# Attention steps of 16 heads: both halves' logits together, products with v next, fill work last; a reordered program start

## The chip, the cores and the metric

The kernel runs on one core of one Trainium2 chip. The metric is device time in microseconds (us) from a single launch, the median of several executions. On one core there is no other die to compare with, so a run counts as fast when it is within 1.5% of the fastest run of the same kernel. The engines are called TensorE (PE in the profile), PEld (TensorE's weight loads), VectorE (DVE), ScalarE (ACT), GpSimd (POOL) and SyncE (SP, used here to issue DMAs). "L405" in a profile line is line 405 of that kernel's file.

## The reference

Four residual layers, A B A B, on 2048 rows of 576 features. Layer A is attention with 32 heads of 18 features; each query sees 8 keys, at distances 0, 2, ..., 14 behind it. Layer B is a gated MLP with a 2048 x 2048 spatial product; the change does not touch it.

```python
def _A_ref(x, wqkv, wo):
    B, S, D = x.shape                      # 1, 2048, 576
    H, W, dil = 32, 8, 2
    qkv = (x @ wqkv).reshape(B, S, 3, H, D // H).transpose(2, 0, 3, 1, 4)
    q, k, v = qkv[0], qkv[1], qkv[2]
    # ... idx = pos - off*dil, masked where negative; kg, vg are gathered keys and values
    logits = jnp.einsum('bhsd,bhswd->bhsw', q, kg) * (D // H) ** -0.5
    attn = softmax(where(mask, logits, -1e9))
    o = jnp.einsum('bhsw,bhswd->bhsd', attn, vg)
    return o.transpose(0, 2, 1, 3).reshape(B, S, D) @ wo

x = A_x
x = x + _A_ref(_layernorm(x), A_wqkv, A_wo)
x = x + _B_ref(_layernorm(x), B_w_in, B_w_sp, B_b_sp, B_w_out)
x = x + _A_ref(_layernorm(x), A_wqkv, A_wo)
x = x + _B_ref(_layernorm(x), B_w_in, B_w_sp, B_b_sp, B_w_out)
```

## The kernel before

Queries are worked in 19 "head-tiles" of up to 112 rows. For each one the kernel multiplies a window of keys with all queries of the tile for every head (the *logits*, with the window pattern packed into the contracted rows, so that the mask comes out of the same matmul), exponentiates the result on ScalarE, and multiplies it with v (the *products*). A ones column in v gives the softmax denominator. The logits matmuls of a head use 32 of the array's 128 rows; the four row groups are written `tile_position=(32*j, 0)`.

The unit of work is a half-step `u` of 8 heads: four of them make a head-tile, and there are 76 in one attention stage. The rest of the attention stage is *fill work*, put by a table between the half-steps: q and k projections (`PG`), v projections (`VW`), output projections (`WO`), layer norms, DMA issues. All engines run in the order in which the program is written here.

```python
def H_tile(self, name):                    # the logits' PSUM tile: two of them
    return self.ps.tile([P, 2, 512], f32, name=name, tag="H", bufs=2)
# ...
def VW(t, hh, dve):                        # v projection and its copy out of PSUM
    nk = tdim(t)[0]
    pv = self.PT_tile([P, 512], f32, "pv", any_bank=False)
    for c in range(5):
        nc.tensor.matmul(pv[:nk, 0:288], lhsT=self.xnT[:, c, QT * t:QT * t + nk],
                         rhs=wv_sb[:, c, hh * 288:(hh + 1) * 288], start=(c == 0), stop=(c == 4))
    evac(v_ext[:nk, t, ...], pv[:nk, 0:288], dve)       # dve: VectorE, else ScalarE
# ...
def L_mm(u):                               # logits of 8 heads into one H tile
    t, hf, jp = half(u)
    L_tiles[u] = L_ps = self.H_tile("L_ps")
    for ftl in range(4):
        for jj in range(2):
            j = 2 * jp + jj                # two of the four row groups
            nc.tensor.matmul(L_ps[:nk, jj, ...], lhsT=kT[32*j:32*j+32, ...], rhs=qT[32*j:32*j+32, ...],
                             start=True, stop=True, tile_position=(32 * j, 0))
# EXP(u): one activation on ScalarE, H tile -> P_bufs[u % 4]
# PV(u): 8 products with v, P_bufs[u % 4] -> O_ps; NORM(u): divide by the denominator (VectorE)
# ...
for t in range(nvw, NT):
    at(4 * t - 4, VW, t, 0, True)          # copy on VectorE
    at(4 * t - 3, VW, t, 1, False)         # copy on ScalarE
# ... PG, WO, layer norms and loads are placed by at() too
L_mm(0)
for u in range(NU):                        # NU = 76
    EXP(u)
    if u + 1 < NU:
        L_mm(u + 1)
    for f, a in table.pop(u, []):          # fill work
        f(*a)
    if u >= 1:
        PV(u - 1)
        if u % 2 == 0:
            NORM(u - 1)
```

At the program's start, GpSimd makes an identity matrix first (for transposes on TensorE), then a window pattern is built, stored on GpSimd's DMA queue and loaded back on ScalarE's, and the layer norms of rows 1024 to 1535 (the "third group") are applied before the first q and k projections. The q and k projections land in a staging tile and go from there into `QK` by DMA, alternating between the GpSimd and the SyncE queue.

The softmax here doesn't subtract the row's maximum and nothing guards it: scores larger than these inputs give would overflow.

## Time and profile before

| | before |
|---|---|
| time, median of 4 runs | 1252.67 us (1252.26 to 1254.16) |
| span of the profiled run, mean granted clock | 1250.7 us, 0.996 |
| TensorE busy | 1204.0 us (96%) |
| first attention stage, first logits to first MLP matmul | 111.1 us |
| second attention stage | 108.5 us |
| first q/k projection, first logits | 21.77 us, 52.67 us |
| TensorE waits, logits for exponentials | 11.6 us in 31 waits |

From the page of the kernel before: each engine's busy time (with share and number of instructions), the granted TensorE clock in tenths for 40 slices of the span, and the chain of waits by engine.

```profile
PE 1204.0 (96%) x8428; PEld 647.5 (52%) x8528; DVE 542.2 (43%) x1202; ACT 388.4 (31%) x609; POOL 277.6 (22%) x371
...
PEclk9899999999999999999999999999999999999999
...
PE 86%; POOL 3%; ACT 3%; issue 3%; DVE 2%; DMA 1%; SPq 1%; POOLq 0%; ACTq 0%; DVEq 0%
```

TensorE bounds the kernel, at nearly full clock. What matters is therefore whether a change gives TensorE less to do or makes it wait.

The waits of TensorE in the kernel before. A line reads: engine, tile and line that waited, what released it, then the total in us, the number of waits and the longest.

```profile
PE L_ps L405 <- ACT P_sb L413: 11.6, 31, 0.8
PE pt L514 <- DVE ln_xn L509: 10.5, 1, 10.5
PE pp L380 <- DMA xnT<-ln_xn: 4.0, 1, 4.0
PE pt L514 <- ACT xnT L516: 3.1, 1, 3.1
```

The attention loop costs TensorE very little waiting: 11.6 us in both stages together. The other three lines are the start: the first transpose runs at 10.5 us, then 3.1 us are lost to a ScalarE copy, and 4.0 us at the end of the start to transposed x.

The loop itself, in the timeline of TensorE in the kernel before. Columns: start in us, length in us, engine, line, operation, output and input by the program's names, their shapes, the number of instructions in the group.

```profile
711.02 0.78 PE L453 MATMUL pw<-wo_sb,oT 128*128 128x288 bf16 x5
711.63 0.35 PE L424 MATMUL O_ps<-v_ext,P_sb 128*128 128x19 bf16 x8
711.92 0.37 PE L405 MATMUL L_ps<-QK 32*128 32x112 bf16 x8
712.22 0.79 PE L358 MATMUL pv<-wv_sb,xnT 128*128 128x288 bf16 x5
```

There are no idle times in brackets, so there are no waits in this piece. A half-step's logits take 0.30 us until the next matmul starts, its products 0.29 us.

ScalarE in the same stage of the kernel before, where the copies of v alternate between the engines. Square brackets hold the idle time before the group and what ended it.

```profile
720.03 0.40 ACT L352 CAST v_ext<-pv 128x288 bf16<-128x288 f32 x1 [0.42 <-PE pv L358]
720.33 3.41 ACT L413 ACTIVATE P_sb<-L_ps 128x896 bf16<-128x896 f32 x4
725.12 0.40 ACT L352 CAST v_ext<-pv 128x288 bf16<-128x288 f32 x1 [1.38 <-PE pv L358]
```

Once per head-tile ScalarE stands up to 1.38 us idle until a v projection is ready to be copied, and then does four exponentials in a row. The period of 5.09 us from copy to copy is TensorE's, not ScalarE's.

Last, the groups of the logits (L405) and the products (L424) in the kernel before: shapes, count, busy us, mean ns of one, idle time before the group and its releasers. The busy times of two groups overlap where one starts before the other has ended (eight logits last 0.37 us, the next matmul starts after 0.30), so they can't be added up exactly.

```profile
L405 PE MATMUL L_ps<-QK 32*128 32x112 bf16 (+1 forms) x1216 | 54.9, 208 | 11.9 <-ACT P_sb L413 11.6
L424 PE MATMUL O_ps<-v_ext,P_sb 128*128 128x19 bf16 (+1 forms) x1216 | 53.8, 172 | 0.0
```

### The profile page before, as it was taken

The page shows a single profiled execution, that of the slowest core. Times are in us where ns is not written, and L with a number is a line of the kernel's source. Part 1 is how long each engine was busy: PE and PEld are TensorE (multiplying, and loading weights), DVE is VectorE, ACT ScalarE, POOL GpSimd, SP SyncE. Part 2 cuts the span into 40 slices and gives each one's busy share as a digit, 9 for nine tenths or more (in the row PEclk, how much of TensorE's full clock was granted, in tenths as well). Part 3 has the DMA queues.
Part 4 walks back from the last instruction along what each step waited for, and adds up shares of the span by engine and source line. Part 5 has one row for each costly group of instructions (what it writes and reads, how often), then busy time and mean ns, then how long its engine had stood idle before and what let it go on. Part 6 is the DMA issues. An engine that isn't in the chain of part 4 may idle for free.

```text
span 1250.7 us, 20588 instructions
## 1 busy us (share of the span) xinstructions
PE 1204.0 (96%) x8428; PEld 647.5 (52%) x8528; DVE 542.2 (43%) x1202; ACT 388.4 (31%) x609; POOL 277.6 (22%) x371
## 2 busy tenths in 40 slices
PE   5799999999999999999998999999999999999998
PEld 3367754444444444447755677444444444444577
DVE  9246658633223323324552567674322332232321
ACT  4366757701110111011146676774011011101000
POOL 2346567400000000001132466772000000000000
PEclk9899999999999999999999999999999999999999
DMA  5678779000000000046644797960000000000342
GB/s 163 119 166 175 155 163 231 4 18 12 11 11 1 11 11 11 1 152 172 174 105 113 169 198 171 193 134 22 1 11 12 11 11 11 11 1 1 125 118 72
DMA packets 175686, 101.56 MB, mean 81 GB/s; under 512 B 134296, under 2 KB 155864, under 8 KB 175592
## 3 DMA queue, kind: packets, MB, share of 16 engines
q1 hardware_dynamic: 163632, 76.70, 27.6%
q0 software_dynamic: 6448, 17.67, 5.4%
q10 hardware_dynamic: 5512, 5.88, 1.5%
q8 instruction: 66, 1.08, 0.3%
q14 instruction: 28, 0.23, 0.1%
HBM read 42.39 MB, written 16.53 MB: 47 GB/s over the span
## 4 chain that ended last, share of the span: by engine, by line
PE 86%; POOL 3%; ACT 3%; issue 3%; DVE 2%; DMA 1%; SPq 1%; POOLq 0%; ACTq 0%; DVEq 0%
PE pg L794 40%; PE pz L776 12%; PE po L848 11%; PE pz L699 10%; PE pp L380 6%; PE pv L358 3%; ACT P_sb L413 2%; POOL ln_xn L235 2%; PE L_ps L405 2%; PE pw L453 2%; PE pzs L699 1%; PE O_ps L424 1%; DVE QK L182 1%; DVE ln_st L497 1%; ACT stg L352 1%
## 5 line engine op out<-in xcount | busy, mean ns | idle before, releaser
L794 PE MATMUL pg<-Wq,Z 128*128 128x512 bf16 x2256 | 500.0, 379 | 2.4
L794 PEld LDWEIGHTS <-Z 128*128 128x128 bf16 x2304 | 225.5, 98 | 271.8
L798 DVE TENSOR_TENSOR g_tmp<-pg,ln_xn 128x512 f32<-128x512 f32 x144 | 99.6, 692 | 429.1 <-PE pg L794 417.2
L788 ACT ACTIVATE z1T<-pz 128x1024 bf16<-128x1024 f32 x72 | 73.7, 1023 | 513.9 <-PE pz L776 513.7
L848 PE MATMUL po<-wout,Z 128*128 128x288 bf16 x1152 | 141.4, 286 | 0.0
L77 POOL DMA_DIRECT2D wout<-in_B_w_out_dram x4 | 4.3, 1064 | 604.6 <-PE pg L794 604.6
L776 PE MATMUL pz<-xnT,w 128*128 128x512 bf16 (+1 forms) x630 | 135.0, 380 | 1.1 <-issue 0.6
L413 ACT ACTIVATE P_sb<-L_ps 128x896 bf16<-128x896 f32 (+1 forms) x152 | 127.5, 893 | 12.1 <-PE L_ps L405 11.8
L848 PEld LDWEIGHTS <-Z 128*128 128x128 bf16 x1152 | 112.7, 98 | 28.8
L699 PEld LDWEIGHTS <-xnT 128*128 128x128 bf16 (+1 forms) x800 | 66.5, 97 | 82.6 <-issue 24.9
L380 PE MATMUL pp<-xnT,wqk_sb 128*128 128x512 bf16 x378 | 96.0, 394 | 10.4 <-DMA xnT<-ln_xn 4.0
L799 DVE TENSOR_TENSOR Z<-g_tmp,z1T 128x512 bf16<-128x512 f32 x144 | 99.7, 692 | 9.7
L699 PE MATMUL pz<-win2a,xnT 128*128 128x512 bf16 x366 | 101.2, 380 | 1.2 <-ACT zp L713 0.8
L776 PEld LDWEIGHTS <-w 128*128 128x128 bf16 (+1 forms) x640 | 51.1, 97 | 80.0 <-issue 27.1
L713 ACT ACTIVATE zp<-pz 128x1024 bf16<-128x1024 f32 x64 | 65.5, 1023 | 45.7 <-PE pz L699 30.2
L235 POOL TENSOR_SCALAR ln_xn<-x_new,ln_mv,ln_rstd 128x576 bf16<-128x576 f32 x32 | 75.5, 2361 | 3.3
L380 PEld LDWEIGHTS <-wqk_sb 128*128 128x128 bf16 x400 | 38.8, 101 | 54.2 <-issue 16.0
L858 DVE TENSOR_TENSOR x_new<-po,xo 128x288 f32<-128x288 f32 (+1 forms) x64 | 28.8, 456 | 87.8 <-PE po L848 87.8
L699 PE MATMUL pz<-win2b,xnT 128*128 128x512 bf16 (+1 forms) x256 | 65.9, 380 | 0.7
L405 PE MATMUL L_ps<-QK 32*128 32x112 bf16 (+1 forms) x1216 | 54.9, 208 | 11.9 <-ACT P_sb L413 11.6
L358 PE MATMUL pv<-wv_sb,xnT 128*128 128x288 bf16 (+1 forms) x380 | 60.6, 294 | 0.2 <-ACT xnT L516 0.2
L715 DVE CUSTOM_DVE_ANT_0 Z<-zp 128x1536 bf16<-128x1536 bf16 x32 | 56.2, 1756 | 7.8 <-ACT zp L713 7.8
(102 smaller groups left out, 932.0 us busy)
## 6 DMA issues: line engine op xcount, KB each, us to landing
xres<-x_new SPq DMA_DIRECT2D x48, 288.0 KB
xo<-xres SPq DMA_DIRECT2D x48, 288.0 KB
wout<-in_B_w_out_dram POOLq DMA_DIRECT2D x4, 1296.0 KB, 10.0
QK<-stg SPq DMA_DIRECT2D x64, 72.0 KB
QK<-stg POOLq DMA_DIRECT2D x64, 72.0 KB, 3.7
w<-in_B_w_in_dram SPq DMA_DIRECT2D x16, 256.0 KB
win2a<-in_B_w_in_dram POOLq DMA_DIRECT2D x12, 288.0 KB, 5.0
wqk_sb<-in_A_wqkv_dram ACTq DMA_DIRECT2D x2, 1152.0 KB
```

Source lines behind the costliest of these rows:

```text
L235: e.tensor_scalar(out=xn[:nrows, 0:D], in0=x_t[:nrows, :], scalar1=mv[:nrows, 0:1], scalar2=rstd[:nrows, 0:1], op0=ALU.subtract, op1=ALU.mult)
L358: nc.tensor.matmul(pv[:nk, 0:288], lhsT=self.xnT[:, c, QT * t:QT * t + nk], rhs=wv_sb[:, c, hh * 288:(hh + 1) * 288], start=(c == 0), stop ...
L380: nc.tensor.matmul(pp[:, :], lhsT=w, rhs=self.xnT[:, c, PADL + cc * 512:PADL + (cc + 1) * 512], start=(c == 0), stop=(c == 4))
L405: nc.tensor.matmul(L_ps[:nk, jj, ftl * QT:ftl * QT + nq], lhsT=kT[32 * j:32 * j + 32, g, QT * t:QT * t + nk], rhs=qT[32 * j:32 * j + 32, g ...
L413: nc.scalar.activation(out=P_bufs[u % 4][:nk, :, :, 0:nq], in_=Lv[:nk, :, :, 0:nq], func=ACT.Exp, scale=scale)
L699: nc.tensor.matmul(pzvs[ci][:, sub * 512:sub * 512 + w], lhsT=self.xnT[r0:r1, c, PADL + i * P:PADL + (i + 1) * P], rhs=win2(c)[r0:r1, c0 + ...
L776: nc.tensor.matmul(pz1s[q // 2][:, q % 2, :], lhsT=w1[r0:r1, c, sub * P:(sub + 1) * P], rhs=self.xnT[r0:r1, c, PADL + q * 512:PADL + (q + ...
L788: nc.scalar.activation(out=z1T[:, q2 * 512:(q2 + 2) * 512], in_=pz1s[q2 // 2][:, :, :].rearrange("p a b -> p (a b)"), func=ACT.Gelu_apprx_ ...
L794: nc.tensor.matmul(pg[:, :], lhsT=Z[:, jj, i, sub * P:(sub + 1) * P], rhs=Wq[q][:, i, :], start=(i == 0), stop=(i == NS - 1))
L798: nc.vector.tensor_tensor(out=tmp[:], in0=pg[:, :], in1=bsp[:, qs], op=ALU.add)
L799: nc.vector.tensor_tensor(out=uT(jj)[:, sub, qs], in0=tmp[:], in1=z1Ts[jj, sub][:, qs], op=ALU.mult)
L848: nc.tensor.matmul(acc[hh], lhsT=uT(j // 2)[:, j % 2, i * P:(i + 1) * P], rhs=wouts[j // NJH][:, j % NJH, hh * 288:(hh + 1) * 288], start= ...
```

## The change

Its intent is to give TensorE larger pieces of one kind. Sixteen logits matmuls in a row use all four row groups, and are followed at once by 16 products, so that the array changes its mode less often. A step `s` is now 16 heads; it takes both H tiles. Fill work comes last in the step. Which engine copies what is changed along with it: all q/k copies within the steps go to VectorE, and in return the v copies of steps below `PG_END` = 14 all go to ScalarE; from then on every second goes to VectorE. In the first attention stage these are steps 4 to 13, in the second 0 to 13.

The start is reordered too: the pattern's store and load go to the SyncE queue, the identity comes after the pattern, 40 matmuls on the identity are to warm the clock, two of three q/k stores go to GpSimd, and the third group's layer norm moves behind the first eight q/k projections.

```diff
-        def L_mm(u):                       # 8 logits, one H tile
-        ...
+        def L_mm(s):
+            t, hf = divmod(s, 2)
+            nk, nq = tdim(t)
+            L_tiles[s] = [self.H_tile("L_ps") for _ in range(2)]
+            for jp in range(2):
+                for ftl in range(4):
+                    g = 4 * hf + ftl
+                    for jj in range(2):
+                        j = 2 * jp + jj
+                        nc.tensor.matmul(L_tiles[s][jp][:nk, jj, ftl * QT:ftl * QT + nq], ...)
 # ... EXP(s): two activations; PV(s): 16 products, then the normalization (cut)
         for t in range(nvw, NT):
-            at(4 * t - 4, VW, t, 0, True)
-            at(4 * t - 3, VW, t, 1, False)
+            for hh in range(2):
+                at(2 * t - 2 + hh, VW, t, hh, 2 * t - 2 + hh >= PG_END and hh == 0)
-            at((k_ * PG_END) // len(pgs), PG, d, qk, cc, k_ % 2 == 0)
+            at((k_ * PG_END) // len(pgs), PG, d, qk, cc, True)
 # ... output projections and layer norms at the corresponding steps (cut)
         L_mm(0)
-        for u in range(NU):
-            EXP(u)
-            if u + 1 < NU:
-                L_mm(u + 1)
-            for f, a in table.pop(u, []):
+        for s in range(NST):               # NST = 38
+            EXP(s)
+            if s + 1 < NST:
+                L_mm(s + 1)
+            PV(s)
+            for f, a in table.pop(s, []):
                 f(*a)
-            if u >= 1:
-                PV(u - 1)
-                if u % 2 == 0:
-                    NORM(u - 1)
 # the start
-            setup_bufs()
             self.build_window_rows(sb)     # its store: SyncE queue instead of GpSimd's
-            self.load_pat(nc.scalar)
+            self.load_pat(nc.sync)
+            self.make_ident()
+            warm = self.PT_tile([P, 512], f32, "warm", any_bank=False)
+            for _ in range(40):
+                nc.tensor.matmul(warm[:, 0:P], lhsT=self.ident[:], rhs=self.ident[:], start=True, stop=True)
+            setup_bufs()
 # ...
-            LNX_apply(*LNX_stats(8, 4))
-            q2 = (nc.gpsimd, nc.sync)
+            q2 = (nc.gpsimd, nc.sync, nc.gpsimd)
             for k_, (d, cc) in enumerate(order):
                 for qk in (1, 0):
                     PG(d, qk, cc, False, q2)
+                if k_ == 3:
+                    LNX_apply(*LNX_stats(8, 4))
```

More of the change, by code (lines that the diff above doesn't have):

```diff
@@ L101, in setup @@
         self.ident = c.tile([P, P], bf16, name="ident")
-        nc.gpsimd.memset(self.ident[:], 0.0)
-        nc.gpsimd.affine_select(out=self.ident[:], in_=self.ident[:], compare_op=ALU.not_equal, fill=1.0,
-                                base=0, pattern=[[-1, P]], channel_multiplier=1)
         self.ones = c.tile([P, 1], bf16, name="ones")
@@ L116, in setup @@
         self.xn_rr = 0
-        for xb in self.xn_bufs:
-            nc.gpsimd.memset(xb[:, D:640], 0.0)
         self.deferred = []
@@ L171, in build_window_rows @@
                                     base=-32 * j - 31, pattern=[[0, PADL]], channel_multiplier=1)
-        self.dma(one[:].rearrange("a r (p f) -> p (a r) f", f=16), R[0:16].rearrange("p a r f -> p (a r) f"), eng=nc.gpsimd)
+        self.dma(one[:].rearrange("a r (p f) -> p (a r) f", f=16), R[0:16].rearrange("p a r f -> p (a r) f"))
         def load(eng):
@@ L177, in build_window_rows, with make_ident @@
         self.load_pat = load
+    def make_ident(self):
+        nc = self.nc
+        for xb in self.xn_bufs:
+            nc.gpsimd.memset(xb[:, D:640], 0.0)
+        nc.gpsimd.memset(self.ident[:], 0.0)
+        nc.gpsimd.affine_select(out=self.ident[:], in_=self.ident[:], compare_op=ALU.not_equal, fill=1.0,
+                                base=0, pattern=[[-1, P]], channel_multiplier=1)
     def fill_window_rows(self, QK, g0, g1):
@@ L390, in PG @@
                              stg[r0 + DH * j7:r0 + DH * (j7 + 1), :, :], eng=queues[dma_rr[0] % len(queues)])
-        def half(u):
-            return u // 4, (u // 2) % 2, u % 2
-        NU = 4 * NT
-        L_tiles, O_tiles = {}, {}
-        def L_mm(u):
-            t, hf, jp = half(u)
-            nk, nq = tdim(t)
-            L_tiles[u] = L_ps = self.H_tile("L_ps")
-            for ftl in range(4):
-                g = 4 * hf + ftl
-                for jj in range(2):
-                    j = 2 * jp + jj
-                    nc.tensor.matmul(L_ps[:nk, jj, ftl * QT:ftl * QT + nq],
-                                     lhsT=kT[32 * j:32 * j + 32, g, QT * t:QT * t + nk],
-                                     rhs=qT[32 * j:32 * j + 32, g, QT * t + PADL:QT * t + PADL + nq],
-                                     start=True, stop=True, tile_position=(32 * j, 0))
@@ L410, in EXP @@
-        def EXP(u):
-            nk, nq = tdim(half(u)[0])
-            Lv = L_tiles.pop(u)[:, :, 0:4 * QT].rearrange("p a (b c) -> p a b c", c=QT)
-            nc.scalar.activation(out=P_bufs[u % 4][:nk, :, :, 0:nq], in_=Lv[:nk, :, :, 0:nq], func=ACT.Exp, scale=scale)
-        def PV(u):
-            t, hf, jp = half(u)
-            if jp == 0:
-                O_tiles[u // 2] = self.O_tile([P, 512], f32, "O_ps")
-            O_ps = O_tiles[u // 2]
-            nk = tdim(t)[0]
-            for ftl in range(4):
-                for jj in range(2):
-                    idx = 4 * ftl + 2 * jp + jj
-                    nc.tensor.matmul(O_ps[:, idx * (DH + 1):(idx + 1) * (DH + 1)], lhsT=P_bufs[u % 4][:nk, jj, ftl, :],
-                                     rhs=v_ext[:nk, t, 16 * hf + idx, :], start=True, stop=True)
@@ L427, in NORM @@
-        def NORM(u):
-            t, hf, _ = half(u)
-            nq = tdim(t)[1]
-            Ov = O_tiles.pop(u // 2)[:, 0:16 * (DH + 1)].rearrange("p (h e) -> p h e", e=DH + 1)
+        NST = 2 * NT
+        L_tiles = {}
+        def L_mm(s):
+            t, hf = divmod(s, 2)
+            nk, nq = tdim(t)
+            L_tiles[s] = [self.H_tile("L_ps") for _ in range(2)]
[4 more added lines that the diff above has]
+                        j = 2 * jp + jj
+                        nc.tensor.matmul(L_tiles[s][jp][:nk, jj, ftl * QT:ftl * QT + nq],
+                                         lhsT=kT[32 * j:32 * j + 32, g, QT * t:QT * t + nk],
+                                         rhs=qT[32 * j:32 * j + 32, g, QT * t + PADL:QT * t + PADL + nq],
+                                         start=True, stop=True, tile_position=(32 * j, 0))
@@ new lines, in EXP, with PV @@
+        def EXP(s):
+            nk, nq = tdim(s // 2)
+            for jp, L_ps in enumerate(L_tiles.pop(s)):
+                Lv = L_ps[:, :, 0:4 * QT].rearrange("p a (b c) -> p a b c", c=QT)
+                nc.scalar.activation(out=P_bufs[(2 * s + jp) % 4][:nk, :, :, 0:nq], in_=Lv[:nk, :, :, 0:nq], func=ACT.Exp,
+                                     scale=scale)
+        def PV(s):
+            t, hf = divmod(s, 2)
+            nk, nq = tdim(t)
+            O_ps = self.O_tile([P, 512], f32, "O_ps")
+            for jp in range(2):
+                for ftl in range(4):
+                    for jj in range(2):
+                        idx = 4 * ftl + 2 * jp + jj
+                        nc.tensor.matmul(O_ps[:, idx * (DH + 1):(idx + 1) * (DH + 1)],
+                                         lhsT=P_bufs[(2 * s + jp) % 4][:nk, jj, ftl, :],
+                                         rhs=v_ext[:nk, t, 16 * hf + idx, :], start=True, stop=True)
+            Ov = O_ps[:, 0:16 * (DH + 1)].rearrange("p (h e) -> p h e", e=DH + 1)
@@ L487, in layer_A @@
             self.zero_right()
+            self.build_window_rows(sb)
+            self.load_pat(nc.sync)
[3 more added lines that the diff above has]
+                nc.tensor.matmul(warm[:, 0:P], lhsT=self.ident[:], rhs=self.ident[:], start=True, stop=True)
             setup_bufs()
-            self.build_window_rows(sb)
-            self.load_pat(nc.scalar)
             def LNX_stats(i0, n):
@@ L553, in layer_A @@
         else:
-            q2 = (nc.gpsimd, nc.sync)
+            q2 = (nc.gpsimd, nc.sync, nc.gpsimd)
             for k_, (d, cc) in enumerate([(d, cc) for d in range(5) for cc in range(2)]):
@@ L576, in layer_A, with at @@
         table = {}
-        def at(u, f, *a):
-            table.setdefault(min(u, NU + 16), []).append((f, a))
-        for t in range(nvw, NT):
-            at(4 * t - 4, VW, t, 0, True)
-            at(4 * t - 3, VW, t, 1, False)
+        def at(s, f, *a):
+            table.setdefault(s, []).append((f, a))
         pgs = [(d, qk, cc) for d, cc in ((0, 2), (1, 2), (0, 3), (1, 3), (2, 2), (2, 3), (3, 2), (3, 3), (4, 2), (4, 3))
                for qk in (1, 0)]
-        PG_END = 30
+        PG_END = 14
         for d, qk, cc in pgs[:4]:
@@ L589, in layer_A @@
         for k_, (d, qk, cc) in enumerate(pgs):
-            at((k_ * PG_END) // len(pgs), PG, d, qk, cc, k_ % 2 == 0)
+            at((k_ * PG_END) // len(pgs), PG, d, qk, cc, True)
+        for t in range(nvw, NT):
+            for hh in range(2):
+                at(2 * t - 2 + hh, VW, t, hh, 2 * t - 2 + hh >= PG_END and hh == 0)
         for i in range(NS):
             t = -(-(i + 1) * P // QT) - 1
-            u = 4 * t + (12 if t < NT - 3 else 10)
-            at(u - 10, XO, i)
-            at(u, WO, i, 0)
-            at(u + 1, WO, i, 1)
-            at(u + 1, LN_STATS, i)
-            at(u + 2, LN_XN, i)
-            at(u + 3, XST, i)
+            s = 2 * t + (4 if t < NT - 3 else 3)
+            at(s - 5, XO, i)
+            at(s, WO, i, 0)
+            at(s + 1, WO, i, 1)
+            at(s + 1, LN_STATS, i)
+            at(s + 2, LN_XN, i)
+            at(s + 2, XST, i)
             if i < NS - 1:
-                at(u + 6, LN_T, i)
+                at(s + 4, LN_T, i)
         if li == 0:
@@ L604, in layer_A @@
         for k_, f in enumerate(self.load_win2a(nc.gpsimd)):
-            at(4 + 3 * k_, f)
-        at(PG_END + 3, alloc_win2b)
+            at(2 + 2 * k_, f)
+        at(PG_END + 2, alloc_win2b)
         for k_ in range(6):
-            at(PG_END + 3 + 3 * k_, win2b_piece, k_)
+            at(PG_END + 2 + 2 * k_, win2b_piece, k_)
         L_mm(0)
-        for u in range(NU):
-            EXP(u)
-            if u + 1 < NU:
-                L_mm(u + 1)
-            for f, a in table.pop(u, []):
-                f(*a)
-            if u >= 1:
-                PV(u - 1)
-                if u % 2 == 0:
-                    NORM(u - 1)
-        PV(NU - 1)
-        NORM(NU - 1)
-        for u in sorted(table):
-            for f, a in table[u]:
+        for s in range(NST):
[4 more added lines that the diff above has]
+            for f, a in table.pop(s, []):
+                f(*a)
+        for s in sorted(table):
+            for f, a in table[s]:
                 f(*a)
```

## The prediction

> **What bounds it now.** TensorE is busy 1204.0 of 1250.7 us (page, part 1), 86% of the chain of waits. The attention stages run 57 to 164 us and 667 to 776 us (timeline). One head-tile (four half-steps) takes 6.5 to 7.0 us while projections are mixed in, then 5.08 us. TensorE's waits for ACT's exponentials total only 11.6 us (waits, TensorE, logits on exponentials). The start loses more: the first transpose at 10.5 us, 3.1 us idle because ACT's queue stands on the window-pattern load, a half-clock spell, and a 4.0 us wait for transposed x at 57 us.
>
> **What the change saves.** Eight logits matmuls use two row groups: 0.165 us of starts plus 0.137 us until a full-array matmul starts. Sixteen in a row (once per layer, at 667.09) take 0.33 us instead of 2 x 0.30. The Trainium skill ("TensorEngine Tiling (Array Packing)", Key Properties) says that changing tiling mode drains the array; the 0.10 to 0.14 us gaps agree. With fewer switches around the products with v, I estimate 0.36 us a step, 76 steps: 27 us of TensorE work.
>
> **What it costs.** A step now takes both H buffers. The logits of step s+1 must wait for the exponentials of step s; before, one half ran ahead. Worse, ACT works in program order (before, it sits 1.38 us per head-tile until a v projection is ready, and only then starts the next exponential). In the new order, ACT gets: exponentials s, copy of v projection s, exponentials s+1. That projection stands on TensorE behind logits s+1, products s and a q/k projection. This closes a serial loop:
> exponential pair 1.71 + hand-over 0.09 + last logits and drain 0.30 + products 0.39 + q/k projection 1.08 + v projection to copy 0.83 + copy 0.30 = 4.7 us per step, against about 3.3 before. After the projections end, every second v copy goes to DVE: steps alternate 3.6 and 2.0, 5.65 us per head-tile against 5.08.
> The copies sit on ACT in steps 4 to 13 of the first attention and 0 to 13 of the second. Adding in-order sums with these durations gives 105 and 107.5 us for before (trace: about 106.5 and 108.5) and 124 and 134.6 us for after: +46 us. TensorE then idles about 2 us in one piece in the early steps. Before, a 2.0 us gap (37.0 to 39.0) was followed by 3.4 us of half clock; "TensorE: Matmul & The Clock Gate" (Part 1) describes such throttling. I add 4 us.
>
> **Start.** ACT no longer stands on the pattern load; 40 matmuls on the identity warm the clock; more q/k stores go to POOL. DVE stays almost as busy, so it gates: I estimate attention starts 7 us earlier (3 to 11).
>
> **Sum.** 1252.5 + 46 + 4 - 7 = 1295 us; range 1279 to 1310. Chances: faster 0.03, same 0.06, slower 0.91.
>
> **Right if:** sixteen logits take about 0.33 us and total logits plus products shrink; TensorE's wait of logits for exponentials grows from 11.6 us to about 80; ACT waits for v projections; steps with projections about 4.7 us, later 5.65 per head-tile; layer B unchanged; the first projection starts about 4 us sooner, attention about 7.
>
> **Wrong if:** logits start before the copies (no serial loop): then TensorE's saving shows and the result is about 1225. If the clock is at half speed in most projection steps, above 1310. If the start stays at 57 us, 7 us more.

## More of the kernel before

Over the whole kernel before, ScalarE's waits for v projections sum to this:

```profile
ACT v_ext L352 <- PE pv L358: 37.9, 40, 1.5
```

## The result, and the profile after

| | before | after |
|---|---|---|
| time, median of 4 runs each | 1252.67 us (1252.26 to 1254.16) | 1304.35 us (1301.1 to 1305.32) |
| ratio of fast runs, 95% interval | 1 | 1.0406 [1.0384, 1.0427] |
| span of the profiled run, granted clock | 1250.7 us, 0.996 | 1301.7 us, 0.979 |
| first q/k projection, first logits | 21.77, 52.67 us | 16.10, 49.63 us |
| first attention stage | 111.1 us | 129.6 us |
| the same, from the first q/k projection inside the steps | 106.7 us | 123.5 us |
| second attention stage | 108.5 us | 146.4 us |
| TensorE waits, logits for exponentials | 11.6 us (31) | 54.0 us (91) |
| ScalarE waits for v projections | 37.9 us (40) | 128.1 us (53) |

Ratios in this document are the mean time of one kernel's fast runs over that of the other's fast runs in the same rounds, so they are not quite the ratios of the medians quoted beside them.

The change cost 4.1%. The spans account for it: first logits 3.0 us earlier, first attention stage 18.5 us longer, second 37.9 us longer, everything between and after them 2.4 us shorter; in sum the 51.0 us by which the two spans differ. Part of the first of these gains is lost again at once: the first q/k projection inside the steps starts at 57.05 us before and 55.77 us after, just 1.3 us earlier, and counted from there the first stage is 16.8 us longer. The MLP layers take no part in it.

The page after, the same three lines:

```profile
PE 1222.9 (94%) x8568; PEld 637.6 (49%) x8568; DVE 549.8 (42%) x1206; ACT 381.4 (29%) x605; POOL 276.2 (21%) x380
...
PEclk9899999999999999999996799999999999999999
...
PE 87%; ACT 8%; DVE 2%; DMA 2%; issue 0%; POOL 0%; SPq 0%; DVEq 0%; ACTq 0%; POOLq 0%
```

TensorE is busy for 18.9 us *more*. Not all of that is real: 4.3 us are the warming matmuls, and 100 matmul records are missing from the trace before (8428 matmuls for 8528 weight loads; after, 8568 and 8568). But two slices, about 683 to 748 us into the span, ran at a granted clock of 0.6 to 0.7. ScalarE's share of the chain of waits went from 3% to 8%.

The wait of TensorE that grew (columns as before):

```profile
PE L_ps L407 <- ACT P_sb L416: 54.0, 91, 2.6
```

Waits of logits for exponentials went up by 42 us. Here is how they look in the timeline of TensorE, one step of the first attention stage:

```profile
91.52 0.37 PE L407 MATMUL L_ps<-QK 32*128 32x112 bf16 x8 [0.36 <-ACT P_sb L416]
92.33 0.37 PE L407 MATMUL L_ps<-QK 32*128 32x112 bf16 x8 [0.44 <-ACT P_sb L416]
92.63 0.56 PE L427 MATMUL O_ps<-v_ext,P_sb 128*128 128x19 bf16 x16
93.05 1.24 PE L383 MATMUL pp<-xnT,wqk_sb 128*128 128x512 bf16 x5
94.12 0.78 PE L361 MATMUL pv<-wv_sb,xnT 128*128 128x288 bf16 x5
95.07 0.77 PE L453 MATMUL pw<-wo_sb,oT 128*128 128x288 bf16 x5 [0.17 <-DVE stg L353]
96.21 0.37 PE L407 MATMUL L_ps<-QK 32*128 32x112 bf16 x8 [0.36 <-ACT P_sb L416]
```

And ScalarE in the same window after:

```profile
90.25 0.40 ACT L355 CAST v_ext<-pv 128x288 bf16<-128x288 f32 x1 [2.66 <-PE pv L361]
90.54 1.73 ACT L416 ACTIVATE P_sb<-L_ps 128x896 bf16<-128x896 f32 x2
94.94 0.40 ACT L355 CAST v_ext<-pv 128x288 bf16<-128x288 f32 x1 [2.66 <-PE pv L361]
```

Read the two together. At 92.63 all sixteen logits have been issued. TensorE goes on with the products, a q/k projection and at 94.12 a v projection. ScalarE could start the next exponentials as soon as the logits are there. It does not: next in its program is the copy of that v projection, which is ready at 94.94. It is idle for 2.66 us, copies, and only at 95.23 starts two exponentials. The first frees an H tile, and the next eight logits start at 96.21. From 91.52 to 96.21 is 4.69 us, and the steps repeat it (86.83, 91.52, 96.21, 100.90). The Trainium skill's page "Perfetto Trace Analysis", section "Tensor Engine Instruction (MATMUL, LD_WEIGHTS)", says that "ACT/DVE/GPSIMD are strict FIFO"; this trace agrees, with 2.66 us of standing behind one copy while other work was ready. In the kernel before, the same habit cost ScalarE 1.38 us per head-tile and TensorE only 0.18 us (a wait at 722.2 us, the one in that head-tile). There one H tile was a half-step ahead; that this lead hid the copy is read from the two traces, and no run gives the lead back with the copies left in place. ScalarE's waits for v projections over the whole kernel after:

```profile
ACT v_ext L355 <- PE pv L361: 128.1, 53, 5.4
```

The logits in a step are not sixteen in a row any more: they come as eight and eight, 0.44 us of waiting between them, since each half waits for its own exponential. The groups of the logits and the products after show it:

```profile
L407 PE MATMUL L_ps<-QK 32*128 32x112 bf16 (+1 forms) x1216 | 49.5, 215 | 56.6 <-ACT P_sb L416 54.0 <-DMA QK<-stg 2.3
L427 PE MATMUL O_ps<-v_ext,P_sb 128*128 128x19 bf16 (+1 forms) x1216 | 42.8, 173 | 0.0
```

The products lost 11.0 us of busy time (53.8 to 42.8), the logits only 5.4 us (54.9 to 49.5).

The granted clock in two windows of the kernel after. Columns: window, its length, busy us (and number) of PE, PEld, DVE, ACT and POOL, granted clock, DMA share, GB/s.

```profile
86.80:105.60 18.80, 14.88 (x190) 9.15 (x190) 9.68 (x25) 8.16 (x13) 9.34 (x11) 1.00 0.56 131
706.10:730.00 23.90, 19.11 (x148) 9.56 (x147) 5.80 (x12) 7.81 (x12) 1.94 (x4) 0.50 0.35 75
```

Both windows have TensorE busy about 80% of the time. The first ran at full clock, the second at half clock throughout its 23.9 us. In the second window of TensorE's timeline after, the same kind of groups takes about double:

```profile
711.65 2.29 PE L383 MATMUL pp<-xnT,wqk_sb 128*128 128x512 bf16 x5
...
716.45 0.56 PE L407 MATMUL L_ps<-QK 32*128 32x112 bf16 x8 [1.31 <-ACT P_sb L416]
```

Five q/k matmuls take 2.29 us instead of 1.24, and a step 6.55 us instead of 4.69. The longest idle time in that window is 1.31 us, in the first window 0.44 us. So the busy share of 94% on the page is partly a slow clock, not work.

### The profile page after: what moved, and what is told of

The parts are those of the page before. It is cut to its first block, busy times and chain, and to the rows that moved or that the text cites. A ratio compares the mean times of both kernels' runs of the same rounds, so it can differ in the third digit from the quotient of the medians.

```text
span 1301.7 us, 20710 instructions
## 1 busy us (share of the span) xinstructions
PE 1222.9 (94%) x8568; PEld 637.6 (49%) x8568; DVE 549.8 (42%) x1206; ACT 381.4 (29%) x605; POOL 276.2 (21%) x380
## 3 DMA queue, kind: packets, MB, share of 16 engines
HBM read 42.39 MB, written 16.53 MB: 45 GB/s over the span
## 4 chain that ended last, share of the span: by engine, by line
PE 87%; ACT 8%; DVE 2%; DMA 2%; issue 0%; POOL 0%; SPq 0%; DVEq 0%; ACTq 0%; POOLq 0%
PE pg L794 38%; PE pz L776 11%; PE po L848 11%; PE pz L699 10%; ACT P_sb L416 6%; PE pp L383 5%; PE pv L361 4%; PE O_ps L427 3%; PE L_ps L407 2%; PE pw L453 1%; PE pzs L699 1%; ACT v_ext L355 1%; DMA x_in<-in_A_x_dram 1%; DVE QK L185 1%; DVE ln_st L501 1%; DMA QK<-stg 0%
## 5 line engine op out<-in xcount | busy, mean ns | idle before, releaser
L416 ACT ACTIVATE P_sb<-L_ps 128x896 bf16<-128x896 f32 (+1 forms) x152 | 124.7, 899 | 8.1 <-PE L_ps L407 8.1
L383 PE MATMUL pp<-xnT,wqk_sb 128*128 128x512 bf16 x400 | 103.5, 412 | 9.2 <-ACT stg L355 6.1
L699 PE MATMUL pz<-win2a,xnT 128*128 128x512 bf16 x384 | 104.1, 380 | 0.0
L407 PE MATMUL L_ps<-QK 32*128 32x112 bf16 (+1 forms) x1216 | 49.5, 215 | 56.6 <-ACT P_sb L416 54.0
L776 PEld LDWEIGHTS <-w 128*128 128x128 bf16 (+1 forms) x640 | 51.1, 97 | 80.0 <-issue 27.1
L407 PEld LDWEIGHTS <-QK 32*128 32x128 bf16 (+1 forms) x1216 | 32.6, 95 | 85.6 <-issue 80.3
L77 POOL DMA_DIRECT2D QK<-stg x74 | 47.9, 651 | 102.2 <-DVE stg L353 45.4
```

Of the source, the lines that this page charges most:

```text
L383: nc.tensor.matmul(pp[:, :], lhsT=w, rhs=self.xnT[:, c, PADL + cc * 512:PADL + (cc + 1) * 512], start=(c == 0), stop=(c == 4))
L407: nc.tensor.matmul(L_tiles[s][jp][:nk, jj, ftl * QT:ftl * QT + nq], lhsT=kT[32 * j:32 * j + 32, g, QT * t:QT * t + nk], rhs=qT[32 * j:32 * ...
L416: nc.scalar.activation(out=P_bufs[(2 * s + jp) % 4][:nk, :, :, 0:nq], in_=Lv[:nk, :, :, 0:nq], func=ACT.Exp, scale=scale)
L699: nc.tensor.matmul(pzvs[ci][:, sub * 512:sub * 512 + w], lhsT=self.xnT[r0:r1, c, PADL + i * P:PADL + (i + 1) * P], rhs=win2(c)[r0:r1, c0 + ...
L776: nc.tensor.matmul(pz1s[q // 2][:, q % 2, :], lhsT=w1[r0:r1, c, sub * P:(sub + 1) * P], rhs=self.xnT[r0:r1, c, PADL + q * 512:PADL + (q + ...
```

## The experiments

The leading theory is the serial loop: the v copy on ScalarE stands between the exponentials of two steps, and its projection is at the end of TensorE's work for the step. Rivals: (1) the step needs both H tiles, so TensorE must stop at every step, wherever the copy is; (2) most of the loss is the half clock; (3) the reordered start contributes. Runs sent together share the runs of the kernel before, whose medians were 1251.93 us (first four), 1252.03 us (next four) and 1251.79 us (last two). The first four ran on one chip, the other six on another, so comparisons across the two groups (e1 with e6; e4 with e7, e9 and e10) go by way of the kernel before, which differed by 0.1 us. All outputs agreed with the reference. A variant of the last pair, four staging tiles without a further edit, did not fit into SBUF and was never run.

### e1_copies_on_dve: the copies leave ScalarE

```diff
-                at(2 * t - 2 + hh, VW, t, hh, 2 * t - 2 + hh >= PG_END and hh == 0)
+                at(2 * t - 2 + hh, VW, t, hh, True)
```

> The changed kernel with one thing different: every copy of a v projection inside the attention steps goes to DVE, so none stands between two exponential pairs on ACT. Theory (serial loop through the copy on ACT): the 4.69 us steps fall to about 3.3, the sums of durations give 96.7 and 98.4 us for the two attentions instead of 124.0 and 134.6, the half-clock spells of the second attention go, and the time is about 1230 us (1222 to 1242), below the kernel before. Rival (the cause is that a step takes both H buffers, so logits cannot run ahead of exponentials, whoever copies): TensorE still waits over 40 us for exponentials and the time stays above 1285 us. DVE, which gets 24 and 24 more copies of 0.38 us, may hold back a few us.

Measured: 1234.33 us (1231.56 to 1240.32), ratio to before 0.9866 [0.9836, 0.9897]. One argument in one line takes 70 us off the changed kernel. The attention stages take 106.8 and 100.6 us (the first 100.0 us from the first projection inside the steps, where the sums expected 96.7; 3.8 us of it are one wait of the first output projection, see e8). TensorE's waits in e1:

```profile
PE L_ps L407 <- ACT P_sb L416: 6.6, 7, 2.6
```

Its logits and products:

```profile
L407 PE MATMUL L_ps<-QK 32*128 32x112 bf16 (+1 forms) x1216 | 35.8, 210 | 9.0 <-ACT P_sb L416 6.6 <-DMA QK<-stg 2.4
L427 PE MATMUL O_ps<-v_ext,P_sb 128*128 128x19 bf16 (+1 forms) x1216 | 43.2, 172 | 0.0
```

Rival (1) falls as a cause by itself: the step still takes both H tiles, and the wait is nearly gone. The intended saving shows here: by these groups 54.9 - 35.8 + 53.8 - 43.2 = 29.7 us less busy time on TensorE for the same matmuls, in the changed kernel only 16.4 us, as the wait split the logits again and part of them ran at half clock. As group times overlap, e6 measures the saving step by step.

### e2_fill_first: the other way to open the loop

The copies stay on ScalarE, but their projections run before the next logits, so ScalarE has its copy's input early.

```diff
         for s in range(NST):
             EXP(s)
+            for f, a in table.pop(s, []):
+                f(*a)
             if s + 1 < NST:
                 L_mm(s + 1)
             PV(s)
-            for f, a in table.pop(s, []):
-                f(*a)
```

> The changed kernel with one thing different: inside a step the fill work (projections, output projection) is issued before the next step's logits and the products, not after. The copies of v stay on ACT. Theory (the loop is made by the order: the projection whose copy ACT waits for stands behind the next logits): the projection now runs while ACT is at the exponentials, the copy is ready when they end, steps with projections take about 3.2 us, the sums give 95.1 and 96.9 us, and the time is about 1227 us (1218 to 1240). Rival 1 (ACT simply has too much to do with 24 and 24 copies): time stays near 1304, because ACT's work is unchanged. Rival 2 (both H buffers in a step): time stays above 1285 us.

Measured: 1256.8 us (1252.43 to 1258.67), ratio 1.0037 [1.0015, 1.0058]. The total missed what was expected by 30 us. The loop did open, as a step in the timeline of TensorE shows (same stage, copies still on ScalarE):

```profile
90.78 0.40 PE L407 MATMUL L_ps<-QK 32*128 32x112 bf16 x16
91.11 0.56 PE L427 MATMUL O_ps<-v_ext,P_sb 128*128 128x19 bf16 x16
...
92.61 0.78 PE L361 MATMUL pv<-wv_sb,xnT 128*128 128x288 bf16 x5
...
94.25 0.40 PE L407 MATMUL L_ps<-QK 32*128 32x112 bf16 x16
```

A step takes 3.5 us (90.78 to 94.25), logits and products without a wait, and the second attention stage went from 146.4 to 102.2 us. What went wrong is elsewhere, in TensorE's waits:

```profile
PE pw L453 <- DMA oT<-o_t: 10.6, 9, 2.3
PE pz L699 <- ACT zp L713: 7.3, 2, 3.6
...
PE L_ps L407 <- ACT P_sb L416: 0.7, 3, 0.3
```

Moving the fill work to the front of its step also moved it ahead of the products of that step, so each output projection now comes before work that used to give its input time: it waits 10.6 us for the transposed attention output (oT). And the last output projections now stand before the last products; the MLP's first matmuls lose 7.3 us to waits for ScalarE, and from the MLP's first matmul to its first spatial product takes 86.7 and 90.5 us, against 83.1 and 82.8 before. The clock took a share that was not separated: in the first stage, from the first projection inside the steps, the granted clock was 0.91 in e2 and 0.98 in e5 below. The Trainium skill's "Perfetto Trace Analysis", section "Optimization Strategy", says that a gap that repeats can mean that there is too little SBUF or PSUM for the next tile. Here the gap that repeated was gone (0.7 us of waits left) with the same two H tiles: its cause was order.

### e3_keep_clock: the serial loop stays, TensorE is kept busy

Matmuls on the identity, with no use for their result, fill the idle time in the steps with a copy on ScalarE.

```diff
+            if s + 1 < NST and (s < PG_END or s % 2 == 1) and 2 * (nvw - 1) <= s < 2 * NT - 2:
+                keep = self.O_tile([P, 512], f32, "keep")
+                for _ in range(16 if s < 6 else 6):
+                    nc.tensor.matmul(keep[:, 0:P], lhsT=self.ident[:], rhs=self.ident[:], start=True, stop=True)
```

> The changed kernel plus dummy matmuls of the identity (16 of 128 columns in steps 0 to 5, else 6, only in steps whose v copy is on ACT), at the end of the fill work, where TensorE idles anyway; their result is read by nobody. Theory (part of the loss is half clock, brought on by the idle pieces): the half-clock spells in the second attention (34 us in all between 685 and 730) go, its first six steps take 4.7 us instead of up to 6.5, and the time falls by about 11 us to 1293 (1286 to 1298) although TensorE does more. Rival (the half clock only shows, and costs nothing because TensorE idles anyway): time within 2 us of 1304, or longer.

Measured: 1292.43 us (1287.98 to 1293.08), ratio 1.0319 [1.0298, 1.034]. The half-clock spells between 692 and 730 us are gone, the second attention stage is 9.9 us shorter than in the changed kernel (136.5 us), the first 1.2 us (128.4 us). A step still takes 4.69 us, now at full clock, so the idle matmuls do not lengthen it; two neighbouring steps in TensorE's timeline of e3:

```profile
691.01 0.37 PE L407 MATMUL L_ps<-QK 32*128 32x112 bf16 x8 [0.41 <-ACT P_sb L416]
...
695.70 0.37 PE L407 MATMUL L_ps<-QK 32*128 32x112 bf16 x8 [0.41 <-ACT P_sb L416]
```

So the half clock that e3 removed was worth about 11 us of the 52, and rival (2) is a part, not the main one. 136.5 us is also close to the 134.6 us that the in-order sum gave without any clock effect.

### e4_start_only: the kernel before with the new start

The edit is the part of the diff under "the start", put on the kernel before; the loop stays as it was.

> The kernel before with only the start of the change (window pattern loaded by the SP queue, identity made later, 40 warming matmuls, the later layer norm of the third group, stores of q and k two thirds on POOL), its attention steps untouched. From the two traces: first q/k projection 5.7 us earlier, first logits 3.0 us earlier, first projection inside the steps 1.3 us earlier. Theory (most of the early gain is given back to waits for staging buffers and transposed x, and the rest counts): 1250 us, that is 1 to 4 us less than before. Rival (the 7 us that I predicted is there, and the changed attention ate it): 1245 to 1247 us.

Measured (5 rounds): 1248.28 us (1247.05 to 1250.75), ratio 0.9974 [0.9959, 0.9989]: about 3 us, not the 7 us of the prediction. The first projection starts 5.2 us earlier (16.53 us), the first logits 3.5 us (49.13 us). The waits of TensorE in e4 show where the rest is lost:

```profile
PE pp L383 <- ACT stg L355: 5.5, 3, 2.2
PE pp L383 <- DMA xnT<-ln_xn: 4.7, 2, 4.2
```

The first projections wait for staging tiles (copied by ScalarE once a DMA has emptied them), and the last ones for transposed x, 4.2 us in one piece at the same place where the kernel before lost 4.0 us.

### e5_projections_earlier: e2 with the output projections one step later

(The label says "earlier"; what is earlier is the fill work of e2. The edit delays the output projections and all that follows them by a step.)

```diff
 # on e2
             s = 2 * t + (4 if t < NT - 3 else 3)
+            s += 1
             at(s - 5, XO, i)
             at(s, WO, i, 0)
```

> The fill-first kernel with the output projection and what hangs on it (layer norm, stores, transposes) one step later, so that only the q/k and v projections stand earlier than in the changed kernel, and the last products of an attention no longer stand behind an output projection that waits for a transpose. Copies of v as in the changed kernel, half of them on ACT. Theory (order alone made the loop; what the fill-first kernel lost was waits of the output projection for transposes): waits of the output projection for transposes fall from 10.6 us to under 4, TensorE no longer waits 7.3 us for the first gelu, the time is about 1232 us (1226 to 1241). Rival (ACT cannot carry the copies): stays at 1250 or more.

Measured: 1225.88 us (1224.19 to 1227.77), ratio 0.9787 [0.977, 0.9805], just past the good end of what was expected (1226 to 1241). The attention stages take 98.1 and 95.8 us. TensorE's waits in e5:

```profile
PE pw L453 <- DMA oT<-o_t: 4.1, 3, 2.0
...
PE L_ps L407 <- ACT P_sb L416: 0.7, 3, 0.3
```

The waits for oT fell from 10.6 to 4.1 us and the MLP's are gone. The rival that ScalarE simply has too much to do falls with it: the copies are all still there. This is the best order found with the copies where the change had put them: 2.1% under the kernel before, 6.0% under the changed kernel (1225.88 / 1304.35 by the medians).

### e6_split_halves: what is the batching worth?

e1, but each step does eight logits, eight products, eight logits, eight products.

```diff
 # on e1; L_mm and PV take the halves to do as an argument (cut)
-            if s + 1 < NST:
-                L_mm(s + 1)
-            PV(s)
+            for jp in range(2):
+                if s + 1 < NST:
+                    L_mm(s + 1, (jp,))
+                PV(s, (jp,))
```

> The kernel with all v copies on DVE, with logits and products dealt in halves again (eight logits, eight products, eight logits, eight products): same work, same dependencies, two more changes between row-tiled and full-array matmuls per step and only two row groups at a time. Theory (batching sixteen logits and sixteen products saves about 0.3 us of TensorE per step): the sums go from 96.7 and 98.4 to 104.3 and 106.7 us (part of the 0.3 us hides where ACT holds the step), so about 1250 us, 12 to 20 us more than the kernel with all copies on DVE of the earlier round (1234). Rival (batching saves nothing): 1234 within 3 us.

Measured: 1246.4 us (1245.47 to 1253.73), ratio 0.9963 [0.9938, 0.9989]; 12.1 us more than e1. The logits and the products in e6:

```profile
L409 PE MATMUL L_ps<-QK 32*128 32x112 bf16 (+1 forms) x1216 | 55.5, 210 | 7.4 <-ACT P_sb L418 4.5 <-DMA QK<-stg 2.6
L433 PE MATMUL O_ps<-v_ext,P_sb 128*128 128x19 bf16 (+1 forms) x1216 | 54.7, 173 | 0.0
```

The busy time of the groups is back at that of the kernel before (55.5 and 54.7 us), so the saving does come from batching. For its size, two neighbouring steps with the same fill work (five v matmuls and five of an output projection), in the timelines of TensorE. In e1:

```profile
125.41 0.40 PE L407 MATMUL L_ps<-QK 32*128 32x112 bf16 x16
...
127.48 0.56 PE L407 MATMUL L_ps<-QK 32*128 32x112 bf16 x16
```

In e6:

```profile
126.75 0.37 PE L409 MATMUL L_ps<-QK 32*128 32x112 bf16 x8
...
129.18 0.37 PE L409 MATMUL L_ps<-QK 32*128 32x112 bf16 x8
```

A step takes 2.07 us in e1 and 2.43 us in e6: 0.36 us saved, an estimated 27 us over 76 steps. In time it is 12 us, as e1 waits more than e6 elsewhere: 3.9 us in the first attention stage and 8.2 us in the second. The two profiled runs differ a little in clock, too (0.990 in e1, 0.995 in e6), so the 12 us may be somewhat too small. The Trainium skill's "TensorEngine Tiling (Array Packing)", section "Key Properties", says that changing the tiling mode drains the array; the gaps in the traces agree (in the kernel before, the next kind of matmul starts 0.14 us after the last of eight logits has started, and logits start 0.10 us after the last product has). But e6 does not test the changes of mode alone, as it also goes back to two row groups at a time. Starts of single matmuls in the trace before suggest the shares: eight logits start within 0.16 us and the sixteen at 667.09 us within 0.19 us, which is about 0.14 of the 0.36 us; the rest would be two gaps fewer a step.

### e7_start_no_warm: e4 without the 40 warming matmuls

```diff
 # on e4
-            warm = self.PT_tile([P, 512], f32, "warm", any_bank=False)
-            for _ in range(40):
-                nc.tensor.matmul(warm[:, 0:P], lhsT=self.ident[:], rhs=self.ident[:], start=True, stop=True)
```

> The start-only kernel without its 40 warming matmuls. The clock is then at half speed during the first transposes and v projections: the first q/k projection starts about 1.5 us later (18.0 us instead of 16.5). Theory (what comes after waits for DMA and DVE anyway): the first logits move by under 0.5 us and the time stays within 1 us of the start-only kernel (ratio to before 0.9974, about 1248 to 1249 us). Rival (the warming counts in full): 1.5 us more, ratio about 0.9986.

Measured (5 rounds): 1248.91 us (1247.46 to 1251.48), ratio 0.9971 [0.9955, 0.9988], the same as e4. Without warming the first projection starts 1.3 us later (17.84 us), and the first logits at 48.96 instead of 49.13 us: the 1.3 us are lost again to the waits that follow.

### e8_wo_earlier: e5 with an earlier load of the output weights

```diff
 # on e5
+                    self.load_wo(nc.scalar)           # before the attention loop, ScalarE's queue
-        if li == 0:
-            at(1, self.load_wo, nc.gpsimd)
```

> As the kernel with the projections earlier, plus the load of the output projection's weights of the first layer issued before the attention, on ACT's queue, not in its second step behind stores on POOL's queue. Theory (the 3.8 to 4.4 us wait of the first output projection is for these weights): that wait goes and the time is about 4 us below the kernel with the projections earlier, about 1228 us. Rival (it waits for the transposed products): no gain; the load may also delay stores and transposes before the attention.

Measured: 1225.76 us (1223.83 to 1228.63), ratio 0.9788 [0.9769, 0.9806], as e5. The expected gain did not come, but e8 could not show it: e5, on which it is built, no longer has the wait that the load was to shorten. That wait is in e1 (3.8 us) and e2 (4.4 us), and the trace of e2 answers the question. In e2 the two transfers of the load were issued at 64.3 and 65.0 us and took at most 8.1 us to land, so the weights were there by about 74 us, and the wait ran from 74.8 to 79.2 us. The weights were not what it waited for.

### e9_ln_group_early: e4 with the third group's layer norm back in its old place

```diff
 # on e4
+            LNX_apply(*LNX_stats(8, 4))
             q2 = (nc.gpsimd, nc.sync, nc.gpsimd)
 # ...
-                if k_ == 3:
-                    LNX_apply(*LNX_stats(8, 4))
```

> The start-only kernel with the third group's layer norm back at its old place in the program, ahead of the first-half projections. Theory (in the start-only kernel the projections wait for staging buffers because POOL's queue holds stores of q and k behind this layer norm's reciprocal root): in this kernel more stores stand behind it, as before the change, and the waits for staging buffers do not shrink; time within 2 us of the start-only kernel (ratio 0.9974), the first logits within 1 us of 49.1 us. Rival (moving the layer norm later is what delays the transposes that the first steps wait for): first projection inside the steps earlier by 2 us or more, ratio about 0.995.

Measured (5 rounds): 1250.19 us (1248.53 to 1252.82), ratio 0.9993 [0.9978, 1.0007]. The time is 1.9 us above e4 by the medians, just within what was expected (2.4 us by the ratios), but the first logits are not: 54.83 us instead of 49.13, with one wait of 8.9 us for a staging tile in the profile. Moving that layer norm is the part of the start without which there is no gain to be seen.

### e10_four_staging: e4 with a fourth staging tile

```diff
 # on e4
-        NSTG = 3 if li == 0 else 4
+        NSTG = 4
-        R = c.tile([P, 2, MR, 16], bf16, name="win_rows")
+        R = c.tile([P, 2, MR, 16], bf16, name="win_rows", bufs=1)    # makes room
```

> The start-only kernel with four staging buffers for q and k in the first attention in place of three (one small table is single-buffered to make room). Theory (the early gain of 5.2 us at the first projection is cut to 3.5 us at the first logits by three waits for staging buffers, 5.5 us in sum): these waits fall under 2 us, the first logits start 3 to 5 us sooner than 49.1 us, but the 4.2 us wait for the transposed last x group then grows by most of it, so the time falls by only 0 to 2 us (ratio 0.996 to 0.9974). Rival (staging alone holds the start): ratio 0.994 or less.

Measured (5 rounds): 1253.95 us (1251.94 to 1255.17), ratio 1.0019 [1.0006, 1.0031]. The waits for staging tiles are gone from TensorE's waits, and waits for transposed x took their place: 8.7 us in three waits, against 4.7 us in two. First logits at 48.57 us, half a microsecond earlier. So the start is limited by the chain that makes transposed x, and a buffer only moves the wait. The time is worse by some 6 us than e4; about 4 us of it lie in the first MLP stage (86.5 us to its first spatial product, 82.6 us in e4). Why is open.

## Why the prediction was right

It said 1295 us, range 1279 to 1310, with 0.91 on slower; 1304.35 us came. The mechanism was right; two smaller terms were not, and the range was wide enough for both. Point by point:

- **The serial loop: right, to 0.02 us in single steps.** It predicted 4.7 us for a step with projections and 5.65 us per head-tile later; the trace has 4.69 us and 5.67 us (117.82 to 123.49). The prediction counts the first stage from its first projection at 57 us; so counted it grew by 16.8 us against 19. With most of the half clock removed (e3), the stages grew by 15.4 and 28.0 us against 19 and 27.1. That the copy's place in ScalarE's order is the cause is shown, not only argued: e1 moves the copy and e2 moves its projection, and either opens the loop. The loop needs a second condition, that no logits run ahead while ScalarE waits; this was argued, not tested.
- **TensorE's saving: right as work, only partly right as time.** The estimate was 0.36 us a step, 27 us of TensorE work; e1 against e6 has 0.36 us a step. In time it is 12 us, and in the changed kernel the two groups lost just 16.4 us of busy time, for the wait split the logits in two again.
- **"TensorE's wait of logits for exponentials grows from 11.6 us to about 80": the direction right, the size not.** It is 54.0 us. The half clock does not explain it: from the end of a v projection to the next logits TensorE has 1.31 us in a step at half clock, and at full clock, in e3, 1.30 us (where the idle matmuls run). About 11 of the 26 us may be the saving that did not come (27 less 16.4 us): a step of fixed length has less to wait when its work is longer. The rest is open.
- **The clock: the term "I add 4 us" was mis-sized.** It measured about 11 us (e3), although the idle pieces of the early steps were 1.31 us and not about 2. Long spells at half speed came, but not in most steps, so the total stayed under 1310.
- **The start: "attention starts 7 us earlier" was mis-sized.** The 57 us it started from is the first projection inside the steps, and that came 1.3 us earlier in the changed kernel (the first logits 3.0 us); by itself the new start is worth 3 us in time (e4). The first projection came 5.7 us earlier (predicted: about 4), but what was won there was waited away, for staging tiles and then for transposed x (e4, e10).
- **Layer B unchanged: right**, 2.4 us less outside the attention stages and the start.

In the sum the predicted +46 +4 -7 = +43 us became 51.0 us in the spans: loop about +44 (16.8 and 37.9 us in the stages, less the 11 us of clock), clock about +11, start -1, the rest -2. The two errors, clock and start, both point the same way. The prediction's "wrong if" was also borne out in the variants: with the loop open it named about 1225, and e5 has 1225.88. That this fits so closely is luck: e1 opens the loop too and has 1234.33, and e5 also moves the output projections.

## What to carry to other kernels

When an in-order engine does two kinds of work, write down in which order it gets them and what each one waits for on the other engine: a small copy whose input is made late in a step can hold up the exponentials that the next step needs, and the loop then takes the sum of all parts instead of the longest. Before reordering TensorE's work for efficiency, check which buffer kept one engine ahead of the other; the change used both logits buffers for one step and lost the half-step of lead that, by the traces, had hidden the copy. The repair can be one argument, but moving work to open one loop (e2) may put other work before its input is ready, so look at all waits after each move.

## What the Trainium skill lacked or had wrong

- "TensorE: Matmul & The Clock Gate", section "HAM oscillation — how this bites in real kernels", gives the rule of no TensorE idle gaps above about 3.4 us. Here the clock was at half for 23.9 us with TensorE 80% busy and no idle time above 1.31 us, and no wait in the attention loops was longer than 2.6 us. The next section, "A second HAM failure mode: psum-queue depth-cycling", does say that frequent short idle times make the clock go up and down, but gives no length or busy share; and another window of the same kernel with the same busy share (79%) ran at full clock. The windows differ in their longest idle time, 1.31 against 0.44 us, and in this trace every half-clock spell inside the attention loops follows, within 7 us, an idle time of 1.3 us or more (in e3, two follow one of 0.97 us); whether that is what decides was not tested. Filling the gaps (e3) was worth 11 us.
- The same page tells in Part 1 how long warming takes and that the ramp costs little in a typical kernel; it does not say that a warmed start can gain nothing at all: 40 warming matmuls brought the first projection 1.3 us forward, and the time did not change (e4 1248.28 us, e7 1248.91 us), as TensorE then waited longer for its inputs.
- "TensorEngine Tiling (Array Packing)", "Key Properties", names the drain at a change of mode without a size. Here the gaps at the changes were 0.14 us (after logits) and 0.10 us (before them), and batching 16 and 16 in place of 8 and 8 took a step from 2.43 to 2.07 us (e6, e1), a part of which comes from using four row groups at once.
- "Perfetto Trace Analysis", "Optimization Strategy", names too little SBUF or PSUM as what a repeating gap can mean. Instruction order on an in-order engine belongs beside it: 54.0 us of repeating waits became 0.7 us with the same buffers (e2).
